# A block-recurrent attention with gated feed-forward: state products on quarter-array tiles, state updates on column tiles behind the attention outputs

## The chip, the cores and the metric

The kernel runs on one core of one Trainium2 chip. The metric is the time of one execution on the device in microseconds (us), as a median over runs. The scale is 2%: faster, same or slower; each ratio comes with a 95% interval.

Engines in the profile: PE is TensorE's matmuls, PEld its weight loads, DVE is VectorE, ACT ScalarE, POOL GpSimd. A product here is one matmul instruction with the weight load that goes with it.

## The reference

Four batches, 8 heads, 768 positions, head size 64. Attention with a decay per head runs over blocks of positions with a state that is carried along; its output `x` (3072 x 512) goes through a gated feed-forward layer. In short form (helper lines cut):

```python
for b in range(nb):                                   # blocks of positions
    intra = einsum('bhic,bhjc->bhij', qb, kb) * Dmask
    intra = einsum('bhij,bhjd->bhid', intra, vb)
    inter = einsum('bhid,bhde->bhie', qb * lam_pow, kv_state)   # the state product
    out[:, :, sl] = intra + inter
    kb_dec = kb * rev_pow                                       # the decayed keys
    kv_state = lam_block * kv_state + einsum('bhsd,bhse->bhde', kb_dec, vb)  # the state update
...
return (sigmoid(x @ w_gate) * (x @ w_val)) @ w_out
```

## The kernel before

It takes 128 positions a step, so six steps (0 to 5), and works on one step's feed-forward while it makes the next step's attention. Two heads of 64 share the 128 rows of the array. The state `Sb` of a head pair is a 128x128 matrix with the two heads on its diagonal and zeros beside them, so that one full-array product serves both:

```python
Sb = stp.tile([128, B, HP, 128], BF16, tag="Sb", name="Sb")      # HP = 4 head pairs

def piece_a(n, bs):                                   # attention output of step n
    for b in bs:
        OP[n, b] = ps_at.tile([128, HP, C], FP32, name="op", tag="ps")
        for hp in range(HP if n > 0 else 0):          # state product, full array
            nc.tensor.matmul(OP[n, b][:, hp, :], lhsT=Sb[:, b, hp, :],
                             rhs=QS[n, b // 2][:, b % 2, hp, :], ...)
    for b in bs:                                      # within the step: column tiles, one head each
        for hp in range(HP):
            for u in range(2):
                us = slice(u * 64, (u + 1) * 64)
                nc.tensor.matmul(OP[n, b][us, hp, :], lhsT=V[n][:, b, 2 * hp + u, :],
                                 rhs=MT[n, b][:, u, hp, :], ...)
    # ... ScalarE copies OP to XT, the input of the feed-forward

def make_kd(n):                                       # decayed keys, one POOL instruction a step
    KD[n] = kdp.tile([128, B, H, D], BF16, tag="kd", name="kd")
    nc.gpsimd.tensor_tensor(out=KD[n], in0=K[n], in1=kds...to_broadcast([128, B, H, D]), op=ALU.mult)

def piece_c(n, bs):                                   # state update: half of cp is thrown away
    for b in bs:
        cp = ps_at.tile([128, HP, 128], FP32, name="cp", tag="ps")
        for hp in range(HP):
            nc.tensor.matmul(cp[:, hp, :], lhsT=KD[n][:, b, 2 * hp:2 * hp + 2, :],
                             rhs=V[n][:, b, 2 * hp:2 * hp + 2, :], ...)
        # ... VectorE adds the diagonal blocks to the faded state sd, into Sb
```

The order of work is written by hand. `gv` is a pair of gate and value products with 512 columns, `gvh` half of one, `t` the transposes, `sc` and `m` scores and mask, `a` the attention output, `c` the state update; the second argument of `t`, `sc`, `m`, `a` and `c` is the batch pair. For step 1:

```python
fade()            # POOL: sd = Sb * decay
make_kd(1)        # POOL
gv(0, 5, 6, 7); t(1, 0); gv(0, 8); sc(1, 0); gv(0, 9); m(1, 0); gv(0, 10)
a(1, 0)
gv(0, 11); t(1, 1); load(2, "qkv", 0, B); transpose_by_dma(2)
gvh(1, 0, 0, 1); sc(1, 1); gvh(1, 0, 2); m(1, 1); gvh(1, 0, 3, 4)
a(1, 1)
gvh(1, 0, 5, 6); gvh(1, 1, 0, 1, 2, 3, 4, 5, 6)
gv(1, 7); c(1, 0); gv(1, 8); c(1, 1)
fade(); make_kd(2); load(3, "qkv", 0, B)
```

## Time and profile before

| | before |
|---|---|
| time, median of 3 runs | 234.06 us (233.78 to 234.13) |
| span in the profile | 231.8 us |
| PE busy | 97% |
| granted TensorE clock, mean | 1.00 |

From the page of the kernel before: the busy time of each engine, two rows of the span in 40 equal slices (a digit is tenths of a slice; 9 is 90% or more; PEclk is the clock that the throttle granted), and the chain of work that ended last, by engine.

```profile
PE 224.9 (97%) x1566; PEld 116.1 (50%) x1566; DVE 106.3 (46%) x186; ACT 80.8 (35%) x147; POOL 84.4 (36%) x73
...
PE   7799999999999999999999999999999999999994
...
PEclk9999999999999999999999999999999999999999
...
PE 91%; POOL 6%; issue 1%; ACT 0%; DVE 0%; POOLq 0%
```

From the first gate product at 17.2 us on, the timeline lists no wait of PE. A matmul's busy time overlaps that of the next one, so cost is read from starts, not from durations. The timeline of PE in the kernel before, around the attention output of step 5. Columns: start in us, length in us, engine, line, operation, out<-in, size of the tile used, sizes of the data, count.

```profile
189.78 0.61 PE L233 MATMUL op<-QS,Sb 128*128 128x128 bf16 x8
190.32 0.64 PE L240 MATMUL op<-MT,vb 128*64 128x128 bf16 x16
190.89 2.76 PE L344 MATMUL po<-WO,ht 128*128 128x512 bf16 x12
193.49 0.61 PE L233 MATMUL op<-QS,Sb 128*128 128x128 bf16 x8
```

Eight full-array state products hold PE from 189.78 to 190.32. Single starts lie 56 ns apart, so the eight need 0.45 us; the other 0.09 us is the change into column tiles. Sixteen column-tiled products take 0.57 us, again 0.45 us for eight pairs and 0.12 us for the way back to the full array. The output products behind them start 2.60 us before the next block: 216 ns each. Half a state update (one batch pair) between gate products, in step 3 of the same timeline:

```profile
127.86 0.61 PE L279 MATMUL cp<-vb,kd 128*128 128x128 bf16 x8
128.31 1.03 PE L299 MATMUL gp<-XT,WG 128*128 128x512 bf16 x4
```

It holds PE for 0.45 us, eight starts of 56 ns, and pays no change of mode.

The timeline of POOL in the same kernel, where it makes the decayed keys `kd` of step 1. In square brackets: idle time before, and what ended it.

```profile
35.80 4.03 POOL L271 TENSOR_TENSOR sd<-Sb,dec 128x512 f32<-128x512 bf16 x4
42.08 3.62 POOL L262 TENSOR_TENSOR kd<-kb,kds 128x2048 bf16<-128x2048 bf16 x1 [2.25 <-DMA kb<-in_k_dram]
```

The keys are ready at 45.70 us. The kernel before first needs them at 58.5 us, so this wait of POOL costs it nothing.

### The profile page before, as it was taken

How to read it: one execution, taken by the hardware profiler on the slowest of the kernel's cores; microseconds unless marked ns; L12 is line 12 of the kernel's file. 1: busy time of each engine (PE TensorE's matmuls, PEld its weight loads, DVE VectorE, ACT ScalarE, POOL GpSimd, SP SyncE). 2: the span in 40 equal slices, each digit the busy share in tenths (PEclk: the TensorE clock that was granted, in tenths of full speed). 3: DMA queues.
4: the chain of work that ended last, by engine and by line, in shares of the span. 5: the costliest groups of instructions: out<-in, count | busy, mean ns of one | idle time of the engine just before them, and what ended most of it. 6: DMA issues, size and time to landing. Idle time of an engine off the chain costs nothing.

```text
span 231.8 us, 3884 instructions
## 1 busy us (share of the span) xinstructions
PE 224.9 (97%) x1566; PEld 116.1 (50%) x1566; DVE 106.3 (46%) x186; ACT 80.8 (35%) x147; POOL 84.4 (36%) x73
## 2 busy tenths in 40 slices
PE   7799999999999999999999999999999999999994
PEld 2444555788544455544455544455544455444442
DVE  4362757554870530845640845840754750243300
ACT  5653343554222224333134243233333223434221
POOL 8999988770596000695000596000000000000000
PEclk9999999999999999999999999999999999999999
DMA  8999999999949992919921919931820012100022
GB/s 57 144 177 174 162 192 158 198 183 156 138 88 120 206 217 75 166 36 134 138 93 45 189 42 113 154 90 53 184 47 0 0 45 93 45 0 0 3 90 91
DMA packets 102465, 24.89 MB, mean 107 GB/s; under 512 B 91568, under 2 KB 99504, under 8 KB 102448
## 3 DMA queue, kind: packets, MB, share of 16 engines
q0 software_dynamic: 82064, 14.16, 83.7%
q1 hardware_dynamic: 20384, 10.49, 20.1%
q8 instruction: 12, 0.20, 0.4%
q14 instruction: 5, 0.04, 0.0%
HBM read 28.32 MB, written 6.29 MB: 149 GB/s over the span
## 4 chain that ended last, share of the span: by engine, by line
PE 91%; POOL 6%; issue 1%; ACT 0%; DVE 0%; POOLq 0%
PE po L344 26%; PE gp L299 24%; PE vp L305 24%; PE vp L322 3%; PE op L240 3%; PE gp L316 3%; PE sp L210 2%; PE op L233 2%; PE cp L279 2%; POOL vb L78 1%; PE po L333 1%; POOL MT L222 1%; POOL qb L78 1%; POOL kb L78 1%; POOL WV L85 1%
## 5 line engine op out<-in xcount | busy, mean ns | idle before, releaser
L308 DVE TENSOR_TENSOR ht<-sg,vp 128x512 bf16<-128x512 bf16 x65 | 44.7, 688 | 85.7 <-PE vp L305 85.4
L305 PE MATMUL vp<-XT,WV 128*128 128x512 bf16 x260 | 66.7, 379 | 0.0
L299 PE MATMUL gp<-XT,WG 128*128 128x512 bf16 x260 | 66.8, 379 | 0.0
L302 ACT ACTIVATE sg<-gp 128x512 bf16<-128x512 f32 x65 | 38.8, 597 | 74.6 <-PE gp L299 74.5
L344 PE MATMUL po<-WO,ht 128*128 128x512 bf16 x276 | 62.6, 380 | 0.0
L344 PEld LDWEIGHTS <-ht 128*128 128x128 bf16 x276 | 25.9, 98 | 30.8
L305 PEld LDWEIGHTS <-WV 128*128 128x128 bf16 x260 | 25.4, 98 | 31.0 <-DMA WV<-in_moe_w_val_dram 0.5
L299 PEld LDWEIGHTS <-WG 128*128 128x128 bf16 x260 | 24.5, 98 | 27.4 <-DMA WG<-in_moe_w_gate_dram 0.4
L271 POOL TENSOR_TENSOR sd<-Sb,dec 128x512 f32<-128x512 bf16 x16 | 16.3, 1038 | 54.0 <-DVE Sb L288 54.0
L227 DVE TENSOR_TENSOR MT<-sp,mask 128x512 bf16<-128x512 f32 x44 | 27.8, 683 | 13.5 <-PE sp L210 13.5
L347 ACT COPY ob<-po 128x512 f32<-128x512 f32 x23 | 13.5, 586 | 52.5 <-PE po L344 48.7
L262 POOL TENSOR_TENSOR kd<-kb,kds 128x2048 bf16<-128x2048 bf16 x5 | 18.1, 3624 | 2.3 <-DMA kb<-in_k_dram 2.3
L247 ACT CAST XT<-op 128x512 bf16<-128x512 f32 x23 | 12.4, 588 | 5.0 <-PE op L240 5.0
L288 DVE TENSOR_TENSOR Sb<-cp,sd 64x256 bf16<-64x256 f32 x32 | 13.5, 420 | 0.8
L78 POOL DMA_DIRECT2D qb<-in_q_dram x9 | 12.4, 1385 | 0.8 <-POOLq L515 0.8
L78 POOL DMA_DIRECT2D vb<-in_v_dram x9 | 12.2, 1360 | 0.0
L78 POOL DMA_DIRECT2D kb<-in_k_dram x8 | 11.5, 1434 | 0.0
L145 PE MATMUL wm<-zero 128*128 128x512 bf16 x26 | 8.9, 477 | 1.2 <-DVE zero L97 1.2
L326 DVE TENSOR_TENSOR ht<-sg,vp 128x256 bf16<-128x256 bf16 x14 | 5.8, 420 | 6.2 <-PE vp L322 3.8
L322 PE MATMUL vp<-XT,WV 128*128 128x256 bf16 x56 | 8.4, 272 | 0.1
L316 PE MATMUL gp<-XT,WG 128*128 128x256 bf16 x56 | 8.4, 273 | 0.0
L240 PE MATMUL op<-MT,vb 128*64 128x128 bf16 x184 | 7.6, 222 | 0.2 <-POOL MT L222 0.2
(62 smaller groups left out, 119.8 us busy)
## 6 DMA issues: line engine op xcount, KB each, us to landing
out_dram<-ob SPq DMA_DIRECT2D x23, 256.0 KB, 2.0
qb<-in_q_dram POOLq DMA_DIRECT2D x4, 512.0 KB, 8.0
kb<-in_k_dram POOLq DMA_DIRECT2D x4, 512.0 KB, 10.0
vb<-in_v_dram POOLq DMA_DIRECT2D x4, 512.0 KB, 13.1
WG<-in_moe_w_gate_dram POOLq DMA_DIRECT2D x6, 256.0 KB, 6.8
WV<-in_moe_w_val_dram POOLq DMA_DIRECT2D x6, 256.0 KB, 7.1
WO<-in_moe_w_out_dram POOLq DMA_DIRECT2D x3, 512.0 KB, 14.2
kb<-in_k_dram POOLq DMA_DIRECT2D x4, 256.0 KB, 6.5
```

What stands on the lines that cost most here:

```text
L78: nc.gpsimd.dma_start(out=t[:, b0:b1], in_=src[b0:b1, :, sl, :].rearrange("b h s d -> s (b h) d"))
L227: nc.vector.tensor_tensor(out=MT[n, b][:, u], in0=SP[n, b][u], in1=mask[:, u], op=ALU.mult)
L240: nc.tensor.matmul(OP[n, b][us, hp, :], lhsT=V[n][:, b, 2 * hp + u, :], rhs=MT[n, b][:, u, hp, :], start=(n == 0 and hp == 0), stop=(hp == ...
L262: nc.gpsimd.tensor_tensor(out=KD[n], in0=K[n], in1=kds.unsqueeze(1).unsqueeze(3).to_broadcast([128, B, H, D]), op=ALU.mult)
L271: nc.gpsimd.tensor_tensor(out=SD[b], in0=Sb[:, b], in1=dec.unsqueeze(2).to_broadcast([128, HP, 128]), op=ALU.mult)
L299: nc.tensor.matmul(gp, lhsT=WG[:, mt, fs], rhs=x[:, mt, :], start=(mt == 0), stop=(mt == NMT - 1))
L302: nc.scalar.activation(sg, gp, AF.Sigmoid)
L305: nc.tensor.matmul(vp, lhsT=WV[:, mt, fs], rhs=x[:, mt, :], start=(mt == 0), stop=(mt == NMT - 1))
L308: nc.vector.tensor_mul(HT[n, ft], sg, vp)
L316: nc.tensor.matmul(gp[:, cs], lhsT=WG[:, mt, fs], rhs=x[:, mt, cs], start=(mt == 0), stop=(mt == NMT - 1))
L322: nc.tensor.matmul(vp[:, cs], lhsT=WV[:, mt, fs], rhs=x[:, mt, cs], start=(mt == 0), stop=(mt == NMT - 1))
L344: nc.tensor.matmul(po, lhsT=HT[n, ft][:, tt * 128:(tt + 1) * 128], rhs=WO[:, ft, :], start=(ft == 0), stop=(ft == NFT - 1))
```

## The change

The intent is to stop computing zeros. The state is kept as 64x64 blocks. A state product becomes four independent quarter-array products (64 rows by 64 columns of the array), which may run at once; for this the heads are paired h and h+2, so that the two row halves and the two column halves belong to different heads. A state update becomes column tiles of 64x64 outputs, half the columns of before. The updates move behind the attention outputs (in step 1 behind those of each batch pair, from step 2 on behind those of both pairs, which now make one block), where the array is in column tiles already. Since h and h+2 do not lie together in memory, queries and keys of steps 2 and later are loaded as even heads and odd heads, and the transposes of steps 0 and 1 become column tiles. With the state half as large, fading it is half the work for POOL.

The core of the diff (loads, transposes, index changes and step 0 are cut):

```diff
-    Sb = stp.tile([128, B, HP, 128], BF16, tag="Sb", name="Sb")
+    Sb = stp.tile([128, B, HP, D], BF16, tag="Sb", name="Sb")
...
+    def head(g, u):
+        return 4 * (g % 2) + 2 * u + g // 2
...
+        for bp in pairs:
+            for i in range(2):
+                for x in range(2):
+                    for u in range(2):
+                        for e in range(2):
+                            nc.tensor.matmul(OP[bp, u][half(e), x, i, :],
+                                             lhsT=Sb[half(u), 2 * bp + i, 2 * e + x, :],
+                                             rhs=QS[n, bp][half(u), e, i, x, :], ...)
...
+    def c(n, *pairs):
+        for bp in pairs:
+            cp = pool.tile([128, 2, HP, D], FP32, name="cp", tag=tag)
+            for i in range(2):
+                for hp in range(HP):
+                    for u in range(2):
+                        h = head(hp, u)
+                        nc.tensor.matmul(cp[half(u), i, hp, :], lhsT=kdh(n, 2 * bp + i, h),
+                                         rhs=V[n][:, 2 * bp + i, h, :], ...)
...
     a(1, 0)
+    c(1, 0)
     gv(0, 11)
...
     a(1, 1)
+    c(1, 1)
     gvh(1, 0, 5, 6)
-    gvh(1, 1, 0, 1, 2, 3, 4, 5, 6)
-    gv(1, 7)
-    c(1, 0)
-    gv(1, 8)
-    c(1, 1)
     fade()
     make_kd(2)
...
-        a(nx, 0)
         piece_po(n, 2)
-        a(nx, 1)
+        a(nx, 0, 1)
+        if nx + 1 < NSTEP:
+            c(nx, 0, 1)
         piece_po(n, 3)
```

More of the change, by code (lines that the diff above doesn't have):

```diff
@@ L74, in load @@
             lst, src = {"q": (Q, q), "k": (K, k), "v": (V, v)}[c]
+            if n > 1 and c != "v":
+                lst[n] = qkv.tile([128, 2, B, HP, D], BF16, tag=c + "b", name=c + "b")
+                for e in range(2):
+                    nc.gpsimd.dma_start(
+                        out=lst[n][:, e].rearrange("p b y d -> p (b y) d"),
+                        in_=src[:, e::2, sl, :].rearrange("b y s d -> s (b y) d"))
+                continue
             if n not in lst:
                 lst[n] = qkv.tile([128, B, H, D], BF16, tag=c + "b", name=c + "b")
-            t = lst[n]
             nc.gpsimd.dma_start(
-                out=t[:, b0:b1],
+                out=lst[n][:, b0:b1],
                 in_=src[b0:b1, :, sl, :].rearrange("b h s d -> s (b h) d"))
@@ L126 @@
         us = slice(u * 64, (u + 1) * 64)
-        nc.scalar.activation(lnp[us, :], lam_bc[us, u::2], AF.Ln)
+        nc.scalar.activation(lnp[us, :].rearrange("p (e x) -> p e x", e=2),
+                             lam_bc[us, :].rearrange("p (x u e) -> p u e x", u=2, e=2)[:, u], AF.Ln)
     lamq = const.tile([128, HP, C], BF16, tag="lamq")
@@ L136, with half, transpose @@
     mask = const.tile([128, 2, HP, C], FP32, tag="mask")
-    nc.vector.tensor_tensor(out=mask, in0=tri.unsqueeze(1).unsqueeze(1).to_broadcast([128, 2, HP, C]),
-                            in1=pk.rearrange("p (g u) -> p u g", u=2).unsqueeze(3).to_broadcast([128, 2, HP, C]),
-                            op=ALU.mult)
+    for u in range(2):
+        nc.vector.tensor_tensor(
+            out=mask[:, u].rearrange("p (e x) c -> p e x c", e=2),
+            in0=tri.unsqueeze(1).unsqueeze(1).to_broadcast([128, 2, 2, C]),
+            in1=pk.rearrange("p (x u e) -> p u e x", u=2, e=2)[:, u].unsqueeze(3).to_broadcast([128, 2, 2, C]),
+            op=ALU.mult)
+    def half(e):
+        return slice(e * 64, (e + 1) * 64)
+    def head(g, u):
+        return 4 * (g % 2) + 2 * u + g // 2
+    def transpose(out, x, b, g):
+        for u in range(2):
+            nc.tensor.transpose(out[half(u)], x[:, b, head(g, u), :], ident)
     wm = ps_ff.tile([128, TCH], FP32, name="wm", tag="ff")
@@ L152, in transpose_by_dma @@
     def transpose_by_dma(n):
-        QR[n] = trsb.tile([128, B, HP, C], BF16, tag="QR", name="QR", bufs=2)
-        kt = trsb.tile([128, B, HP, C], BF16, tag="KR", name="KR", bufs=2)
+        QR[n] = trsb.tile([128, 2, B, 2, C], BF16, tag="QR", name="QR", bufs=2)
+        kt = trsb.tile([128, 2, B, 2, C], BF16, tag="KR", name="KR", bufs=2)
         for dst, src in ((QR[n], Q[n]), (kt, K[n])):
-            nc.sync.dma_start_transpose(out=dst.rearrange("p b g c -> p (b g) c"),
-                                        in_=src.rearrange("p b h d -> p (b h d)"))
@@ L158, in transpose_by_dma, with scale @@
-        for bp in range(2):
-            KS[n, bp] = kt[:, 2 * bp:2 * bp + 2]
+            nc.sync.dma_start_transpose(out=dst.rearrange("p e b x c -> p (e b x) c"),
+                                        in_=src.rearrange("p e b y d -> p (e b y d)"))
+        for bp in range(NB2):
+            KS[n, bp] = kt[:, :, 2 * bp:2 * bp + 2]
+    lamq_e = lamq.rearrange("p (e x) c -> p e (x c)", e=2)
+    def scale(n, bp, src):
+        QS[n, bp] = trsb.tile([128, 2, 2, 2, C], BF16, tag="QS", name="QS")
+        nc.vector.tensor_tensor(out=QS[n, bp].rearrange("p e i x c -> p e i (x c)"),
+                                in0=src.rearrange("p e i x c -> p e i (x c)"),
+                                in1=lamq_e.unsqueeze(2).to_broadcast([128, 2, 2, 2 * C]), op=ALU.mult)
@@ L161, in piece_tq0 @@
     def piece_tq0(bs):
-        tq = ps_at.tile([128, 2, HP, C], BF16, name="tq", tag="ps")
+        tq = ps_at.tile([128, 2, 2, 2 * C], BF16, name="tq", tag="ps")
         for b in bs:
             if (0, b // 2) not in QS:
-                QS[0, b // 2] = trsb.tile([128, 2, HP, C], BF16, tag="QS", name="QS")
-            for hp in range(HP):
-                nc.tensor.transpose(tq[:, b % 2, hp, :], Q[0][:, b, 2 * hp:2 * hp + 2, :], ident)
+                QS[0, b // 2] = trsb.tile([128, 2, 2, 2, C], BF16, tag="QS", name="QS")
+            for g in range(HP):
+                transpose(tq[:, b % 2, g // 2, g % 2 * C:g % 2 * C + C], Q[0], b, g)
@@ L168, in piece_tq0 @@
         for b in bs:
-            nc.vector.tensor_tensor(out=QS[0, b // 2][:, b % 2], in0=tq[:, b % 2], in1=lamq, op=ALU.mult)
+            nc.vector.tensor_tensor(out=QS[0, b // 2][:, :, b % 2].rearrange("p e x c -> p e (x c)"),
+                                    in0=tq[:, b % 2], in1=lamq_e, op=ALU.mult)
     def piece_tk0(bp):
-        tk = ps_at.tile([128, 2, HP, C], BF16, name="tk", tag="ps")
+        tk = ps_at.tile([128, 2, 2, 2 * C], BF16, name="tk", tag="ps")
         for i in range(2):
-            for hp in range(HP):
-                nc.tensor.transpose(tk[:, i, hp, :], K[0][:, 2 * bp + i, 2 * hp:2 * hp + 2, :], ident)
@@ L176, in piece_tk0 @@
-        KS[0, bp] = trsb.tile([128, 2, HP, C], BF16, tag="KS", name="KS")
+            for g in range(HP):
+                transpose(tk[:, i, g // 2, g % 2 * C:g % 2 * C + C], K[0], 2 * bp + i, g)
+        KS[0, bp] = trsb.tile([128, 2, 2, 2, C], BF16, tag="KS", name="KS")
         for i in range(2):
-            nc.scalar.copy(KS[0, bp][:, i], tk[:, i])
+            nc.scalar.copy(KS[0, bp][:, :, i].rearrange("p e x c -> p e (x c)"), tk[:, i])
     def piece_t(n, bp):
         if n > 1:
-            QS[n, bp] = trsb.tile([128, 2, HP, C], BF16, tag="QS", name="QS")
-            nc.vector.tensor_tensor(out=QS[n, bp], in0=QR[n][:, 2 * bp:2 * bp + 2],
-                                    in1=lamq.unsqueeze(1).to_broadcast([128, 2, HP, C]), op=ALU.mult)
+            scale(n, bp, QR[n][:, :, 2 * bp:2 * bp + 2])
@@ L185, in piece_t @@
             return
-        tq = ps_at.tile([128, 2, HP, C], BF16, name="tq", tag="ps")
-        tk = ps_at.tile([128, 2, HP, C], BF16, name="tk", tag="ps")
+        tq = ps_at.tile([128, 2, 2, 2, C], BF16, name="tq", tag="ps")
+        tk = ps_at.tile([128, 2, 2, 2, C], BF16, name="tk", tag="ps")
         for i in range(2):
-            for hp in range(HP):
-                nc.tensor.transpose(tq[:, i, hp, :], Q[n][:, 2 * bp + i, 2 * hp:2 * hp + 2, :], ident)
-        QS[n, bp] = trsb.tile([128, 2, HP, C], BF16, tag="QS", name="QS")
@@ L192, in piece_t @@
-        nc.vector.tensor_tensor(out=QS[n, bp], in0=tq,
-                                in1=lamq.unsqueeze(1).to_broadcast([128, 2, HP, C]), op=ALU.mult)
+            for g in range(HP):
+                transpose(tq[:, g // 2, i, g % 2, :], Q[n], 2 * bp + i, g)
+        scale(n, bp, tq)
         for i in range(2):
-            for hp in range(HP):
-                nc.tensor.transpose(tk[:, i, hp, :], K[n][:, 2 * bp + i, 2 * hp:2 * hp + 2, :], ident)
-        KS[n, bp] = trsb.tile([128, 2, HP, C], BF16, tag="KS", name="KS")
+            for g in range(HP):
+                transpose(tk[:, g // 2, i, g % 2, :], K[n], 2 * bp + i, g)
@@ L198, in piece_t @@
+        KS[n, bp] = trsb.tile([128, 2, 2, 2, C], BF16, tag="KS", name="KS")
         nc.scalar.copy(KS[n, bp], tk)
-    SP, OP = {}, {}
+    SP = {}
     def piece_s(n, bs, pool=ps_at, tag="ps"):
@@ L209, in piece_s @@
                     us = slice(u * 64, (u + 1) * 64)
-                    nc.tensor.matmul(sp[u][:, hp, :], lhsT=KS[n, bp][us, i, hp, :],
-                                     rhs=QS[n, bp][us, i, hp, :],
+                    nc.tensor.matmul(sp[u][:, hp, :], lhsT=KS[n, bp][us, hp // 2, i, hp % 2, :],
+                                     rhs=QS[n, bp][us, hp // 2, i, hp % 2, :],
                                      start=(hp == 0), stop=(hp == HP - 1), skip_group_check=True)
@@ L227, in piece_m, with intra @@
             nc.vector.tensor_tensor(out=MT[n, b][:, u], in0=SP[n, b][u], in1=mask[:, u], op=ALU.mult)
-    def piece_a(n, bs):
-        for b in bs:
-            OP[n, b] = ps_at.tile([128, HP, C], FP32, name="op", tag="ps")
-            for hp in range(HP if n > 0 else 0):
-                nc.tensor.matmul(OP[n, b][:, hp, :], lhsT=Sb[:, b, hp, :],
-                                 rhs=QS[n, b // 2][:, b % 2, hp, :],
-                                 start=(hp == 0), stop=False, skip_group_check=True)
-        for b in bs:
-            for hp in range(HP):
-                for u in range(2):
-                    us = slice(u * 64, (u + 1) * 64)
-                    nc.tensor.matmul(OP[n, b][us, hp, :], lhsT=V[n][:, b, 2 * hp + u, :],
-                                     rhs=MT[n, b][:, u, hp, :],
-                                     start=(n == 0 and hp == 0), stop=(hp == HP - 1),
-                                     skip_group_check=True)
+    def intra(n, b, out, m, start, stop):
+        for e in range(2):
+            nc.tensor.matmul(out[half(e)], lhsT=V[n][:, b, 2 * m + e, :],
+                             rhs=MT[n, b][:, m % 2, 2 * e + m // 2, :],
+                             start=start, stop=stop, skip_group_check=True)
@@ new lines, in piece_a @@
+    def piece_a(n, pairs):
+        OP = {(bp, u): ps_at.tile([128, 2, 2, C], FP32, name="op", tag="ps")
+              for bp in pairs for u in range(2)}
+        for bp in pairs:
+            for i in range(2):
+                for x in range(2):
+                    for u in range(2):
+                        for e in range(2):
+                            nc.tensor.matmul(OP[bp, u][half(e), x, i, :],
+                                             lhsT=Sb[half(u), 2 * bp + i, 2 * e + x, :],
+                                             rhs=QS[n, bp][half(u), e, i, x, :],
+                                             start=(i == 0 and x == 0), stop=False,
+                                             skip_group_check=True)
+        for bp in pairs:
+            for u in range(2):
+                for i in range(2):
+                    for x in range(2):
+                        intra(n, 2 * bp + i, OP[bp, u][:, x, i, :], 2 * x + u, False, i == 1 and x == 1)
@@ L244, in piece_a @@
         if n not in XT:
             XT[n] = xtp.tile([128, NMT, B, C], BF16, tag="XT", name="XT")
-        for b in bs:
-            nc.scalar.copy(XT[n][:, :, b, :], OP[n, b])
-    def piece_a0(b):
-        halves = [ps_at.tile([128, 2, C], FP32, name="op", tag="ps") for g in range(2)]
-        for hp in range(HP):
-            for u in range(2):
-                us = slice(u * 64, (u + 1) * 64)
-                nc.tensor.matmul(halves[hp // 2][us, hp % 2, :], lhsT=V[0][:, b, 2 * hp + u, :],
-                                 rhs=MT[0, b][:, u, hp, :], start=(hp % 2 == 0), stop=(hp % 2 == 1),
-                                 skip_group_check=True)
-        nc.vector.tensor_copy(XT[0][:, 0:2, b, :], halves[0])
-        nc.scalar.copy(XT[0][:, 2:4, b, :], halves[1])
@@ L260, in make_kd, with piece_a0 @@
-    def make_kd(n):
-        KD[n] = kdp.tile([128, B, H, D], BF16, tag="kd", name="kd")
-        nc.gpsimd.tensor_tensor(
-            out=KD[n], in0=K[n],
-            in1=kds.unsqueeze(1).unsqueeze(3).to_broadcast([128, B, H, D]), op=ALU.mult)
+        for bp in pairs:
+            for u in range(2):
+                nc.scalar.copy(XT[n][:, u::2, 2 * bp:2 * bp + 2, :], OP[bp, u])
+    def piece_a0(b, split=False):
+        if 0 not in XT:
+            XT[0] = xtp.tile([128, NMT, B, C], BF16, tag="XT", name="XT")
+        w = 2 if split else NMT
+        for m0 in range(0, NMT, w):
+            op = ps_at.tile([128, w, C], FP32, name="op", tag="ps")
+            for m in range(w):
+                intra(0, b, op[:, m, :], m0 + m, m == 0, m == w - 1)
+            if split and m0 == 0:
+                nc.vector.tensor_copy(XT[0][:, m0:m0 + w, b, :], op)
+            else:
+                nc.scalar.copy(XT[0][:, m0:m0 + w, b, :], op)
@@ new lines, in make_kd @@
+    def make_kd(n):
+        if n < 2:
+            KD[n] = kdp.tile([128, B, H, D], BF16, tag="kd", name="kd")
+            nc.gpsimd.tensor_tensor(
+                out=KD[n], in0=K[n],
+                in1=kds.unsqueeze(1).unsqueeze(3).to_broadcast([128, B, H, D]), op=ALU.mult)
+            return
+        KD[n] = kdp.tile([128, 2, B, HP, D], BF16, tag="kd", name="kd")
+        for e in range(2):
+            nc.gpsimd.tensor_tensor(
+                out=KD[n][:, e], in0=K[n][:, e],
+                in1=kds[:, e::2].unsqueeze(1).unsqueeze(3).to_broadcast([128, B, HP, D]), op=ALU.mult)
@@ L266 @@
     SD = {}
     def fade():
-        for b in range(B):
-            SD[b] = kdp.tile([128, HP, 128], FP32, tag="sd", name="sd", bufs=4)
-            nc.gpsimd.tensor_tensor(out=SD[b], in0=Sb[:, b],
-                                    in1=dec.unsqueeze(2).to_broadcast([128, HP, 128]),
+        for bp in range(NB2):
+            SD[bp] = kdp.tile([128, 2, HP, D], FP32, tag="sd", name="sd", bufs=2)
+            nc.gpsimd.tensor_tensor(out=SD[bp], in0=Sb[:, 2 * bp:2 * bp + 2],
+                                    in1=dec.unsqueeze(1).unsqueeze(3).to_broadcast([128, 2, HP, D]),
@@ L273, in fade, with kdh @@
                                     op=ALU.mult)
-    def piece_c(n, bs):
-        for b in bs:
-            cp = ps_at.tile([128, HP, 128], FP32, name="cp", tag="ps")
-            for hp in range(HP):
-                nc.tensor.matmul(cp[:, hp, :], lhsT=KD[n][:, b, 2 * hp:2 * hp + 2, :],
-                                 rhs=V[n][:, b, 2 * hp:2 * hp + 2, :],
-                                 start=(hp == 0), stop=(hp == HP - 1), skip_group_check=True)
-            sd = SD.pop(b, None)
-            for u in range(2):
-                us = slice(u * 64, (u + 1) * 64)
-                if n == 0:
-                    nc.vector.tensor_copy(Sb[us, b, :, us], cp[us, :, us])
-                else:
-                    nc.vector.tensor_tensor(out=Sb[us, b, :, us], in0=cp[us, :, us],
-                                            in1=sd[us, :, us], op=ALU.add)
+    def kdh(n, b, h):
+        return KD[n][:, b, h, :] if n < 2 else KD[n][:, h % 2, b, h // 2, :]
@@ new lines, in c @@
+    def c(n, *pairs):
+        for bp in pairs:
+            pool, tag = (ps_at, "ps") if bp == 0 else (ps_ff, "ff")
+            cp = pool.tile([128, 2, HP, D], FP32, name="cp", tag=tag)
+            for i in range(2):
+                for hp in range(HP):
+                    for u in range(2):
+                        h = head(hp, u)
+                        nc.tensor.matmul(cp[half(u), i, hp, :], lhsT=kdh(n, 2 * bp + i, h),
+                                         rhs=V[n][:, 2 * bp + i, h, :], start=(i == 0 and hp == 0),
+                                         stop=(i == 1 and hp == HP - 1), skip_group_check=True)
+            dst = Sb[:, 2 * bp:2 * bp + 2]
+            if n == 0:
+                nc.vector.tensor_copy(dst, cp)
+            else:
+                nc.vector.tensor_tensor(out=dst, in0=cp, in1=SD.pop(bp), op=ALU.add)
@@ L375 @@
     idle(3)
-    piece_a(0, [0])
-    piece_a(0, [1])
+    piece_a0(0)
+    piece_a0(1)
     idle(2)
-    piece_a(0, [2])
-    piece_a0(3)
+    piece_a0(2)
+    piece_a0(3, True)
     idle(2)
@@ L392 @@
         load_wo(i, NFT // 3)
-    def c(n, bp):
-        piece_c(n, [2 * bp, 2 * bp + 1])
     def t(n, bp):
@@ L405, in m, with a @@
         piece_m(n, 2 * bp + 1)
-    def a(n, bp):
-        piece_a(n, [2 * bp, 2 * bp + 1])
+    def a(n, *pairs):
+        piece_a(n, pairs)
     def gv(n, *fts):
@@ L416, in gvh @@
             piece_gvh(n, ft, i)
-    gv(0, 0, 1, 2, 3)
-    c(0, 0)
-    gv(0, 4)
-    c(0, 1)
+    gv(0, 0, 1, 2, 3, 4)
+    c(0, 0, 1)
     fade()
@@ L450 @@
     load(3, "qkv", 0, B)
-    gv(1, 9, 10, 11)
+    gvh(1, 1, 0, 1, 2, 3, 4, 5, 6)
+    gv(1, 7, 8, 9, 10, 11)
     piece_po(0, 0)
@@ L463 @@
     piece_po(1, 1)
-    a(2, 0)
     piece_po(1, 2)
-    a(2, 1)
+    a(2, 0, 1)
+    c(2, 0, 1)
     piece_po(1, 3)
@@ L476 @@
         transpose_by_dma(nx)
-        gv(n, 0)
-        c(n, 0)
-        gv(n, 1)
-        c(n, 1)
+        gv(n, 0, 1)
         if nx + 1 < NSTEP:
```

## The prediction

> **What bounds it now.** TensorE. The page gives PE 97% busy, the chain of waits is 91% PE, and the granted clock is 1.00. From the first gate product at 17.2 us to the end the PE timeline has no hole: 512-column products start every 216 ns. So PE work saved or added after that, and every new PE wait, goes straight into the time; DVE (46%), ACT and POOL have slack. The first 17 us hang on POOL and loads; I expect 0 to +0.3 us there.
>
> **What the timeline prices.**
> - State product `op<-QS,Sb`: 8 full-array products in 0.45 us (56 ns each) for two batches. As 16 quarter-array ones, four at a time, I estimate 0.22 us. Row-tiled (`sp`) and column-tiled (`op<-MT,vb`) products already run in pairs every 56 ns.
> - State update `cp`: 8 products in 0.447 us. As 16 column tiles of 64 columns, in pairs at about 29 ns (my estimate: half the columns), 0.24 us.
> - Each change of tiling costs about 0.11 us: a pair block takes 0.55 to 0.57 where its columns need 0.45, and the neighbours lose as much. The Trainium skill, "TensorEngine Tiling (Array Packing)", Key Properties, says that changing the mode drains TensorE; the trace agrees in kind.
>
> **Sum on PE.** In steps 2 to 4, attention output plus update goes from 3.13 us to about 2.15 (one block with three mode changes, not two blocks with two each): -0.98 each, -2.9. Last attention output: -0.6. Step 1: -0.7, but the two transposes become column tiles inside full-array work: +0.46. Step 0's update: -0.2. Together about **-3.9 us**.
>
> **The new wait.** The change moves the update of step 1 to right behind its attention output: its first half, from 58.5 us to about 39.7 us. It needs the decayed keys `kd` of step 1. POOL's timeline shows these start at 42.08 us, when the last `kb` load lands (2.3 us idle, released by that DMA), and take 3.62 us, to 45.7. They are one instruction for all batches, and nothing moves that load. The order of PE's instructions has the update waiting for Pool there. PE executes in order, so it stands from 39.6 to 45.8: **+6.1 us**.
>
> **The clock.** At the start products come every 427 ns until 6.4 us, then every 216: half rate. The Trainium skill, "TensorE: Matmul & The Clock Gate", Part 1, describes windows of 3.4 us, an idle one halving the clock until a busy one. The trace agrees at the start. A 6 us hole should do the same, at half rate for some 3 to 6 us: **+2.0 us** (estimate; 0 if it keeps its clock).
>
> Later updates (steps 2 to 4) have `kd` over 10 us early; PSUM buffers come free in time but for perhaps 0.1 us.
>
> **Prediction.** 234.1 - 3.9 + 6.1 + 2.0 + 0.2 = **238.5 us**, 8 in 10 within 236.0 to 241.0. Faster by over 2%: 0.03; within 2%: 0.54; slower by over 2%: 0.43.
>
> **What would show it.** Right: a 6 us hole in PE near 40 us, ended by Pool `kd`; products at 427 ns for some us behind it; quarter tiles in 0.22 us per two batches, updates in 0.24. Wrong: no hole, or a hole without the slow products; quarter tiles at 0.45 us (loads or issue limiting), which would add 2 us; updates at 56 ns a pair, 2 us more.
>
> **What would make it wrong.** The keys landing earlier than at 42 us; a clock that survives the hole (then 236.5); quarter tiles that serialise (then up to 242).

## More of the kernel before

The runs e1 to e4 were made on one chip and e5 to e8 on another, each beside runs of the kernel before in the same rounds.

## The result, and the profile after

| | before | after |
|---|---|---|
| time, median | 233.99 us (4 runs) | 237.53 us (4 runs, 237.17 to 238.21) |
| ratio to before | | 1.0156 (1.0131 to 1.0180) |
| span in the profile | 231.8 us | 235.7 us |
| PE busy | 97% | 95% |
| granted clock, mean | 1.000 | 0.986 |

A ratio here is the mean time of one kernel's runs over the mean of the other's of the same rounds, so it is not quite the ratio of the medians in the table. The changed kernel is 1.6% slower, which is "same" on the 2% scale, but the interval is clear of 1.

The lines of the page of the changed kernel that answer to those of before:

```profile
PE 223.4 (95%) x1790; PEld 112.1 (48%) x1790; DVE 95.5 (41%) x157; ACT 80.5 (34%) x147; POOL 81.7 (35%) x76
...
PE   7789999299999999999999999999999999999994
...
PEclk9999999689999999999999999999999999999999
...
PE 79%; POOL 13%; DMA 5%; issue 1%; DVE 0%; POOLq 0%
```

Slices are 5.9 us wide. In the eighth, from 41.2 us, PE was busy 2 tenths; the clock drops in the same slice and the next. The chain that ended last now runs through POOL and a DMA. PE's timeline of the changed kernel at that place:

```profile
39.79 0.42 PE L268 MATMUL op<-QS,Sb 64*64 64x128 bf16 x16
40.14 0.64 PE L256 MATMUL op<-MT,vb 128*64 128x128 bf16 x16
45.51 0.64 PE L330 MATMUL cp<-vb,kd 128*64 128x64 bf16 x16 [4.74 <-POOL kd L300]
46.09 1.89 PE L346 MATMUL gp<-XT,WG 128*128 128x512 bf16 x4
47.77 1.87 PE L352 MATMUL vp<-XT,WV 128*128 128x512 bf16 x4
49.57 0.64 PE L159 MATMUL tq<-ident,qb 128*64 128x128 bf16 x16
```

PE stands still for 4.74 us, from the attention output of step 1's first batch pair to its state update. Behind the hole, four gate products take 1.68 us (46.09 to 47.77) and four value products 1.80 us, where four took 0.86 us before. POOL's timeline of the changed kernel shows what the hole waits for:

```profile
35.85 2.04 POOL L315 TENSOR_TENSOR sd<-Sb,dec 128x512 f32<-128x512 bf16 x2
41.84 3.62 POOL L300 TENSOR_TENSOR kd<-kb,kds 128x2048 bf16<-128x2048 bf16 x1 [3.94 <-DMA kb<-in_k_dram]
```

The decayed keys are ready at 45.46 us, as early as before (45.70). What changed is who is waiting. Fading the states takes half as long, and all that POOL does with it is wait longer for the key load.

The gain is there as well. PE's timeline of the changed kernel in step 2's attention, both batch pairs and the update in one block:

```profile
93.10 0.64 PE L268 MATMUL op<-QS,Sb 64*64 64x128 bf16 x32
93.67 1.08 PE L256 MATMUL op<-MT,vb 128*64 128x128 bf16 x32
94.59 0.67 PE L330 MATMUL cp<-vb,kd 128*64 128x64 bf16 x32
95.19 2.12 PE L391 MATMUL po<-WO,ht 128*128 128x512 bf16 x9
```

From 93.10 to 95.19 are 2.09 us, with 0.09 us of entry (lost at the end of the output products ahead) 2.18. The kernel before spends two blocks of 1.12 and two updates of 0.447 on the same, 3.13 us.

### The profile page after: what moved, and what is told of

Its sections match the earlier page's. It is cut to its first block, busy times and chain, and to the rows that moved or that the text cites. A ratio compares the mean times of both kernels' runs of the same rounds, so it can differ in the third digit from the quotient of the medians.

```text
span 235.7 us, 4288 instructions
## 1 busy us (share of the span) xinstructions
PE 223.4 (95%) x1790; PEld 112.1 (48%) x1790; DVE 95.5 (41%) x157; ACT 80.5 (34%) x147; POOL 81.7 (35%) x76
## 4 chain that ended last, share of the span: by engine, by line
PE 79%; POOL 13%; DMA 5%; issue 1%; DVE 0%; POOLq 0%
PE po L391 26%; PE gp L346 20%; PE vp L352 20%; DMA kb<-in_k_dram 5%; POOL kd L300 3%; PE gp L363 3%; PE vp L369 3%; PE sp L235 2%; PE op L256 2%; POOL qb L84 2%; POOL WV L91 2%; POOL WG L90 2%; POOL vb L84 2%; POOL kb L84 1%; PE po L380 1%; PE op L268 1%
## 5 line engine op out<-in xcount | busy, mean ns | idle before, releaser
L346 PE MATMUL gp<-XT,WG 128*128 128x512 bf16 x260 | 67.7, 383 | 0.8 <-DMA WG<-in_moe_w_gate_dram 0.8
L352 PE MATMUL vp<-XT,WV 128*128 128x512 bf16 x260 | 67.6, 383 | 0.0
L315 POOL TENSOR_TENSOR sd<-Sb,dec 128x512 f32<-128x512 bf16 x8 | 8.2, 1044 | 54.6 <-DVE Sb L337 54.6
L337 DVE TENSOR_TENSOR Sb<-cp,sd 128x512 bf16<-128x512 f32 x8 | 5.3, 688 | 20.9 <-PE cp L330 20.9
L282 ACT CAST XT<-op 128x512 bf16<-128x512 f32 x20 | 10.4, 597 | 3.0 <-PE op L256 3.0
L306 POOL TENSOR_TENSOR kd<-kb,kds 128x1024 bf16<-128x1024 bf16 x6 | 11.3, 1905 | 0.0
L78 POOL DMA_DIRECT2D qb<-in_q_dram x8 | 9.4, 1184 | 0.0
L78 POOL DMA_DIRECT2D kb<-in_k_dram x8 | 9.2, 1167 | 0.0
L300 POOL TENSOR_TENSOR kd<-kb,kds 128x2048 bf16<-128x2048 bf16 x2 | 7.3, 3629 | 4.0 <-DMA kb<-in_k_dram 3.9
L330 PE MATMUL cp<-vb,kd 128*64 128x64 bf16 x160 | 3.8, 201 | 4.7 <-POOL kd L300 4.7
```

The costliest lines, as they stand in the source:

```text
L78: nc.gpsimd.dma_start(out=lst[n][:, e].rearrange("p b y d -> p (b y) d"), in_=src[:, e::2, sl, :].rearrange("b y s d -> s (b y) d"))
L300: nc.gpsimd.tensor_tensor(out=KD[n], in0=K[n], in1=kds.unsqueeze(1).unsqueeze(3).to_broadcast([128, B, H, D]), op=ALU.mult)
L346: nc.tensor.matmul(gp, lhsT=WG[:, mt, fs], rhs=x[:, mt, :], start=(mt == 0), stop=(mt == NMT - 1))
L352: nc.tensor.matmul(vp, lhsT=WV[:, mt, fs], rhs=x[:, mt, :], start=(mt == 0), stop=(mt == NMT - 1))
```

## The experiments

Eight kernels were run, in two groups, all correct. The theory: the loss comes from the order alone (the update waits for keys that depend on the last key load) and from the clock, which halves in the hole; the tiles gain what was predicted. The main rival: the smaller tiles cost more than they save.

| run | what it is | median, us | ratio to before (95%) |
|---|---|---|---|
| e1_late_update | changed kernel, step 1's update later | 230.42 | 0.9851 (0.9834 to 0.9868) |
| e2_split_keys | changed kernel, step 1's keys in two instructions | 230.97 | 0.9873 (0.9852 to 0.9894) |
| e3_fill_hole | changed kernel, hole filled with products on zeros | 236.12 | 1.0083 (1.0062 to 1.0104) |
| e4_move_alone | kernel before, step 1's update earlier | 242.70 | 1.0368 (1.0333 to 1.0404) |
| e5_update_apart | e1, updates of steps 2 to 4 apart | 231.93 | 0.9905 (0.9874 to 0.9936) |
| e7_tile_by_tile | e1, quarter products in another order | 230.74 | 0.9846 (0.9810 to 0.9882) |
| e8_two_blocks | e1, attention outputs in two blocks | 232.00 | 0.9916 (0.9882 to 0.9951) |
| e6_full_transposes | e1, step 1's transposes full-array | 231.04 | 0.9869 (0.9833 to 0.9905) |

### e1_late_update: take the wait away by order

```diff
     a(1, 0)
-    c(1, 0)
     gv(0, 11)
...
     a(1, 1)
-    c(1, 1)
+    c(1, 0, 1)
```

> The changed kernel with both halves of step 1's state update moved behind the second attention output of step 1 (about 48 us), nothing else. Theory (the update waits for the decayed keys, and the clock halves in that hole): no hole near 40 us, no 427 ns products, so 237.5 - 4.9 - 1.8 = 230.8 us, about 0.986 of the kernel before. Rival (the smaller tiles themselves cost more than they save, and the hole only took up slack that would show elsewhere): 235 us or more, with a new wait.

Measured: 230.42 us, ratio 0.9851. PE's timeline of this run at the new place of the update:

```profile
39.62 0.64 PE L256 MATMUL op<-MT,vb 128*64 128x128 bf16 x16
40.19 1.04 PE L346 MATMUL gp<-XT,WG 128*128 128x512 bf16 x4
...
48.64 0.64 PE L256 MATMUL op<-MT,vb 128*64 128x128 bf16 x16
49.11 0.67 PE L330 MATMUL cp<-vb,kd 128*64 128x64 bf16 x32
49.72 0.61 PE L363 MATMUL gp<-XT,WG 128*128 128x256 bf16 x4
```

No hole and no slow products: four gate products take 0.87 us (40.19 to 41.06, where the value products start). The rival that blamed the tiles falls. This version beats both kernels: 3.5 us (1.5%) faster than before, which is still "same" on the 2% scale but with an interval clear of 1, and 7 us faster than the change as it was.

### e2_split_keys: take the wait away by size

```diff
-            nc.gpsimd.tensor_tensor(
-                out=KD[n], in0=K[n], ...)
+            for bs in (slice(0, 2), slice(2, 4)) if n == 1 else (slice(0, B),):
+                nb = bs.stop - bs.start
+                nc.gpsimd.tensor_tensor(
+                    out=KD[n][:, bs], in0=K[n][:, bs], ...)
```

> The changed kernel with the order kept, but the decayed keys of step 1 made in two POOL instructions, one for each batch pair. Theory (the wait is for one instruction that covers all batches and so hangs on the last key load): the first half needs only the load that lands at 30.8 us and is ready at about 39.8 us, before the update's first half; no hole, 230.8 us as in the late update. Rival (the place behind the attention output is bad in itself, through state or buffer waits): a hole of some us stays near 40 us and the time stays over 234 us.

Measured: 230.97 us, ratio 0.9873; e1 and e2 are not told apart. POOL's timeline, then PE's, of this run:

```profile
38.47 1.90 POOL L302 TENSOR_TENSOR kd<-kb,kds 128x1024 bf16<-128x1024 bf16 x1
42.41 1.90 POOL L302 TENSOR_TENSOR kd<-kb,kds 128x1024 bf16<-128x1024 bf16 x1 [2.05 <-DMA kb<-in_k_dram]
```

```profile
40.93 0.64 PE L256 MATMUL op<-MT,vb 128*64 128x128 bf16 x16
41.40 0.42 PE L332 MATMUL cp<-vb,kd 128*64 128x64 bf16 x16
```

The first half of the keys is ready at 40.37 us and the update starts at 41.40, straight behind the attention output. (PE came about 0.8 us later than in the changed kernel's profile, since this run's first gate product started only at 18.7 us.) The place was never wrong in itself. One POOL instruction over all batches had tied the first pair's update to the second pair's key load.

### e3_fill_hole: keep the hole, take its idleness away

```diff
     a(1, 0)
+    warm = ps_ff.tile([128, TCH], FP32, name="warm", tag="ff")
+    for i in range(20):
+        nc.tensor.matmul(warm, lhsT=zero[:, :128], rhs=zero, start=True, stop=True,
+                         skip_group_check=True)
     c(1, 0)
```

> The changed kernel with 20 full products on zeros (4.3 us at 216 ns) put into the hole, in front of step 1's first update. Theory (TensorE's clock halves because it stood idle): the update still starts when the keys are ready, near 45.5 us, but the products behind it come every 216 ns; 237.5 - 1.8 = 235.7 us. Rival (the slow products behind the hole come from something else at that time, such as the loads): products at 427 ns remain and the time stays 237.5 us.

Measured: 236.12 us, ratio 1.0083. Against the change's 1.0156 that is 0.0073 of 234 us, 1.7 us, give or take 0.8 by the two intervals. The stretches from 36 to 42.5, 42.5 to 49.5 and 49.5 to 56 us, first of the changed kernel, then of this one. Columns: stretch, its length, busy time (and count) of PE, PEld, DVE, ACT and POOL, granted clock, DMA share, GB/s.

```profile
36.00:42.50 6.50, 4.78 (x60) 2.34 (x54) 4.22 (x7) 2.27 (x4) 2.56 (x3) 1.00 2.28 164
42.50:49.50 7.00, 3.99 (x24) 1.54 (x24) 0.69 (x1) 0.60 (x1) 7.00 (x5) 0.51 1.30 203
49.50:56.00 6.50, 6.50 (x101) 5.27 (x104) 4.94 (x10) 2.83 (x6) 3.30 (x3) 1.00 2.42 157
```

```profile
42.50:49.50 7.00, 5.90 (x69) 3.03 (x68) 1.63 (x3) 0.60 (x1) 6.99 (x4) 1.00 1.27 206
```

With the hole filled the clock stays at 1.00, with the loads running as before (206 against 203 GB/s), so the loads are not the cause. The useless products cost no time of their own: they were done before the keys were ready. PE's timeline of this run:

```profile
40.59 4.49 PE L476 MATMUL warm<-zero 128*128 128x512 bf16 x20
46.18 0.44 PE L330 MATMUL cp<-vb,kd 128*64 128x64 bf16 x16 [1.10 <-POOL kd L300]
```

The keys still end the hole, in this run at 46.18 us, because the last key load landed 0.7 us later (POOL started on the keys at 42.51 us). This is no fix, but it prices the second half of the loss.

### e4_move_alone: the order without the tiles

```diff
     a(1, 0)
+    c(1, 0)
     gv(0, 11)
...
     a(1, 1)
+    c(1, 1)
     gvh(1, 0, 5, 6)
...
-    gv(1, 7)
-    c(1, 0)
-    gv(1, 8)
-    c(1, 1)
...
```

This is the kernel before, on full-array tiles; the fading and the next keys follow the second update, as in the change.

> The kernel before, full-array tiles and all, with only the two halves of step 1's update moved to where the change has them. Theory: the hole comes from the order alone; it runs from 39.9 to 45.7 us, 5.8 us, and halves the clock for 1.8 us more: 234.0 + 7.6 = 241.6 us, about 1.032 of the kernel before. Rival (the loss comes with the tiles): 234 to 235 us.

Measured: 242.70 us, ratio 1.0368. PE's timeline of this run:

```profile
39.64 0.64 PE L240 MATMUL op<-MT,vb 128*64 128x128 bf16 x16
45.83 1.03 PE L279 MATMUL cp<-vb,kd 128*128 128x128 bf16 x8 [5.55 <-POOL kd L262]
46.65 1.91 PE L299 MATMUL gp<-XT,WG 128*128 128x512 bf16 x4
```

The same hole, 0.8 us longer because PE arrives at it 0.5 us earlier and the keys come 0.3 us later, and the same slow products behind it (1.71 us for four) on a kernel without one new tile. The order alone loses 8.6 us here by the ratio, 1.0 more than expected. Behind the hole the clock stayed low for 5.0 us in this run's trace, against 4.0 in that of the changed kernel, which at half rate explains half of that; the rest is within the scatter of the runs (241.48 to 243.32).

### e5_update_apart and e8_two_blocks: what sharing a block is worth

e5 puts the updates of steps 2 to 4 back among the gate products; e8 splits the attention outputs of steps 2 to 5.

```diff
 e5 (step 2's update, ahead of the loop, goes in the same way)
-        gv(n, 0, 1)
+        gv(n, 0)
+        c(n, 0)
+        gv(n, 1)
+        c(n, 1)
...
         a(nx, 0, 1)
-        if nx + 1 < NSTEP:
-            c(nx, 0, 1)
         piece_po(n, 3)
```

```diff
 e8 (and the same for step 2, ahead of the loop)
         piece_po(n, 1)
+        a(nx, 0)
         piece_po(n, 2)
-        a(nx, 0, 1)
+        a(nx, 1)
```

> The late-update kernel with the state updates of steps 2 to 4, still column tiles, put back where the kernel before had them: in two halves, between full-array gate products. Theory (each block of smaller tiles pays a change of mode going in and coming out, about 0.1 us each; behind the attention outputs the update finds the array already in column tiles): per step two blocks of about 0.45 us instead of 0.48 us more in a shared block, +0.4 us for each of 3 steps, so 230.4 + 1.3 = 231.7 us. Rival (only the size of the tiles counts, the place gives nothing): 230.4 us.

> The late-update kernel with the attention outputs of steps 2 to 5 in two blocks of one batch pair each, an output block between them, as the kernel before has them; the update stays behind the second. Theory: three more changes of mode a step (full to quarter, quarter to column, column to full), about 0.1 us each, in 4 steps: +1.3 us, 231.7 us. Rival (changes of mode are hidden behind the weight loads): 230.4 us.

Measured: 231.93 us for e5, 0.0054 of 234 us or 1.3 us over e1 by the ratios. 232.00 us for e8, 0.0065 or 1.5 us over e1. Neither interval overlaps that of e1. As e1 ran on the other chip, e7 below, which differs from e1 only in the order of the quarter products and ran in the rounds of e5 and e8, is the better yardstick: its slowest run took 230.98 us, the fastest of e5 and e8 231.60. The traces show the cause. PE's timeline in step 2 of e5, then of e8:

```profile
86.38 1.08 PE L256 MATMUL op<-MT,vb 128*64 128x128 bf16 x32
87.40 2.76 PE L391 MATMUL po<-WO,ht 128*128 128x512 bf16 x12
...
91.82 0.44 PE L330 MATMUL cp<-vb,kd 128*64 128x64 bf16 x16
92.19 1.04 PE L346 MATMUL gp<-XT,WG 128*128 128x512 bf16 x4
```

```profile
83.31 0.42 PE L268 MATMUL op<-QS,Sb 64*64 64x128 bf16 x16
83.66 0.64 PE L256 MATMUL op<-MT,vb 128*64 128x128 bf16 x16
84.23 2.76 PE L391 MATMUL po<-WO,ht 128*128 128x512 bf16 x12
```

Half an update alone holds PE for 0.37 us (91.82 to 92.19) and costs 0.10 us of entry before it: 0.93 us for two halves, where the whole update in the shared block takes 0.60 (94.59 to 95.19 above). The attention output ahead takes 0.10 us more as well, since it now pays the way back to the full array (1.02 us, 86.38 to 87.40, against 0.92). Together 0.43 us more per step, for three steps. In e8 the first block runs from 83.31 to 84.23, 0.92 us plus entry: three changes of mode of about 0.11 us that the joined block does not have, for four steps. The rival, that the changes of mode are hidden, falls.

These lines also say what the tiles would be worth without the shared block, as an estimate that no run checks: two blocks as in e8 (0.92 us and 0.1 of entry each) and two half updates as in e5 (0.93 together) make 2.97 us a step, only some 0.2 less than the 3.13 of the kernel before, where the shared block needs 2.18. So most of the 0.95 us a step hangs on small tiles and shared block together. The full-array tiles in a shared block were not run.

### e7_tile_by_tile: does the order of issue matter

```diff
-            for i in range(2):
-                for x in range(2):
-                    for u in range(2):
-                        for e in range(2):
+            for u in range(2):
+                for e in range(2):
+                    for i in range(2):
+                        for x in range(2):
                             nc.tensor.matmul(OP[bp, u][half(e), x, i, :], ...)
```

> The late-update kernel with the 16 quarter-array state products of a batch pair issued tile by tile (four in a row on the same quarter) instead of round the four quarters. Theory (four run at once only if neighbours in the order are on different quarters; on one quarter each waits 56 ns for the one ahead): 16 take about 0.69 us (only the change of quarter overlaps) to 0.89 us (nothing does) instead of 0.22; over ten pairs +4.7 to +6.7 us, 235 to 237 us. Rival (TensorE picks products of free quarters out of its queue): 0.22 us and 230.4 us.

Measured: 230.74 us, ratio 0.9846, the same as e1. Here my theory fell and the rival held. PE's timeline of this run in step 2:

```profile
86.35 0.69 PE L268 MATMUL op<-QS,Sb 64*64 64x128 bf16 x32
86.97 1.08 PE L256 MATMUL op<-MT,vb 128*64 128x128 bf16 x32
```

32 quarter products took 0.62 us instead of 0.57, not 1.4 or more. The single records of the trace also show how: the first four start 13 ns apart, and the third to start carries the wait that the program has on its ninth product, the first of the third quarter; it is so in all ten batch pairs. Compiled again, this kernel still holds the sixteen products in the order of its source, so it was not the compiler that moved them. So products of different quarters start out of program order, and issue order need not be spread by hand. Of the small rest (0.05 us for two pairs) 0.03 is the spread of a group of four, whose last starts 40 ns after its first, against 10 in e1.

### e6_full_transposes: an attempt at a better version

```diff
-            if n > 1 and c != "v":
+            if n > 0 and c != "v":
...
-                transpose(tq[:, g // 2, i, g % 2, :], Q[n], 2 * bp + i, g)
+                nc.tensor.transpose(tq[:, g // 2, i, g % 2, :],
+                                    Q[n][:, g // 2, 2 * bp + i, 2 * (g % 2):2 * (g % 2) + 2, :], ident)
```

The first pair of lines keeps even and odd heads apart from step 1 on; the transposes of the keys change in the same way, and loads and decayed keys of step 1 follow the new layout. A first attempt that left the loads as they were, and gave the two heads as one strided weight, did not build: the weight must have a single free dimension.

> An attempt at a better kernel: the late-update kernel with step 1's queries and keys loaded in the order of steps 2 and later (even heads, then odd heads, two loads each), so that heads h and h+2 lie together and step 1's transposes are full-array again. Theory: two blocks of transposes shrink from 1.12 to 0.89 us, -0.45 us, 230.0 us, if the last key load, issued some 2 us later by POOL, still lands near 42 us where the second transposes need it; if it lands later, a wait of up to 1 us takes the gain back.

Measured: 231.04 us with a wide scatter (230.01 to 232.36, 6 runs), ratio 0.9869; not told apart from e1. In its trace the transposes of a batch pair take 0.90 us without changes of mode, as in the kernel before, and the key load came in time. The gain on PE is real and small, and these runs do not show it in the time. e1 stays the version to take.

### What stays open

The first gate product started at 17.2 us before and at 18.0 us in the changed kernel's profile. In the profiles the first gate weights are issued at 10.4 us and land after anything from 6.4 us (before) to 8.3 us (e2); the changed kernel had 7.5. e1, e5 and e8 start with the same code as the changed kernel; there the load took 6.5 to 6.8 us and the first gate product started at 17.1 to 17.2. So the later start is scatter of that load and not the change. Why it scatters was not tested.

## Why the prediction was right or wrong

The time (237.53) lay in the range, one microsecond under the predicted 238.5, and the reasons held. That it came so close is in part luck: the tiles gained 0.4 us less than predicted, while the hole and the clock cost 1.4 and 0.3 less, and these errors partly offset each other. Point by point:

- **PE is the bound, and PE time is kernel time.** Right. Without the hole (e1) the smaller tiles and the shared blocks give 3.5 us.
- **Minus 3.9 us from the tiles.** Right in kind, 0.4 us too much. Per step from 2 to 4 the prediction had 0.98 us; the step from one score block to the next went from 35.53 us (110.58 to 146.12 before) to 34.59 (109.74 to 144.33 in e1), 0.94 us. Quarter products start 13.7 ns apart on average (four within 10 ns, then the next four after 56), so 16 need 0.22 us as estimated. The column tiles of the update start 15.3 ns apart on average (in pairs, every 32), so 16 need 0.25 us, where 0.24 was estimated. A change of mode costs about 0.09 to 0.13 us. Some 0.2 us goes to a wait after step 1's update that the prediction put at 0.1: in e1 a half-width gate product that could start at 50.60 us starts at 50.80. The likely cause, not tested: the update holds one of the three buffers of the feed-forward in PSUM (where matmuls put their results), and ScalarE, busy with the two attention copies until 50.17, has read the next one only at 50.75.
- **A hole at 40 us, ended by the keys.** Right, shown by taking it away in two ways (e1, e2) and by making it alone (e4). Its size was off: 4.7 us, predicted 6.1. The term that was mis-sized is the moment at which PE arrives. The hole's end is fixed by POOL (predicted 45.8, measured 45.5), so the 0.84 us that this run lost at its start, and the 0.2 us that the last product still ran after it was issued, came out of the hole; the keys 0.3 us earlier make up the rest. Delay ahead of a wait with a fixed end is free, so it should not have been summed. "PE executes in order" held where it was needed: no gate product started ahead of the waiting update. e7 shows that it is not strictly so between quarters.
- **The clock halves in the hole.** Right: 0.51 granted in the stretch behind, 1.7 us by e3, predicted 2.0. The Trainium skill, "TensorE: Matmul & The Clock Gate", Part 1, has windows of 3.4 us; the trace's slow stretch lasted 6.83 us (42.64 to 49.47), two of them. It began 1.9 us after PE's last product ended: here the clock fell before PE had been idle for a whole 3.4 us, which is less than the idle window that the prediction took from the page. In two of the four timed runs the mean clock was 0.993 and not 0.986, which by its size is about half that stretch at half rate, so this term varies from run to run.
- **Later updates have their keys in time.** Right: PE has no hole behind that one.

## What to carry to other kernels

When work moves earlier on a full engine, ask for every operand when it is ready, not only whether it once was: the slack that an operand had in the old place is invisible in the old profile, except as idle time of an engine off the critical path. When later work stays behind the one that waits, as on PE here, the missing slack becomes a hole, and here the hole of 4.7 us cost about a third more through the clock. Small tiles paid here when neighbouring work shared their mode, since each change cost 0.1 us; and before a good idea with a bad time is dropped, move the one piece that waits.

## What the Trainium skill lacked or had wrong

- "TensorE: Matmul & The Clock Gate", Part 3, says that matmuls start and end strictly in program order. In e7, with four products in a row on each quarter, the third product to start carried the wait of the program's ninth in each of ten batch pairs, and 16 products took about 0.22 us plus 0.03 instead of the 0.69 or more that strict order gives. Whether products on one quarter keep their order is not shown either way.
- "TensorEngine Tiling (Array Packing)", Key Properties, says that a change of mode drains TensorE and gives no figure. Here a change cost about 0.09 to 0.13 us, between full array, row tiles, column tiles and quarters alike.
- "TensorE: Matmul & The Clock Gate", Back-to-back issue gap, gives about 81 ns a matmul with 128 columns and 131 ns with 512 as the sustained rate of weight load and matmul pairs. Here every matmul had its own weight load, and starts lay 56 ns and 216 ns apart, which are the figures that the same section keeps for an isolated gap.
